# The order table covers the whole program, and the second 768-token block's output goes by seven products

## The chip, the cores and the metric

The kernel runs on one core of one Trainium2 chip. The metric is the device time of that core in microseconds, median of several runs. The engines named below are TensorE (PE, its weight loads PEld), VectorE (DVE), ScalarE (ACT), GpSimd (POOL) and SyncE (SP), whose queue issues nearly all DMA transfers.

## The reference

Attention over pooled keys and values, then a feed-forward layer with a gate:

```python
k_p = k.reshape(B, H, Sp, 8, D).mean(axis=3)      # 576 keys -> 72
v_p = v.reshape(B, H, Sp, 8, D).mean(axis=3)
scores = scale * np.matmul(q, k_p.transpose(0, 1, 3, 2))
scores = scores - np.max(scores, axis=-1, keepdims=True)
attn = np.exp(scores)
attn = attn / (np.sum(attn, axis=-1, keepdims=True) + 1e-09)
x = np.matmul(attn, v_p)                          # -> [4608 tokens, 512]
h = x @ w_in                                      # 512 x 2048
g = h * np.clip(h + 3.0, 0.0, 6.0) / 6.0
out = g @ w_out                                   # 2048 x 512
```

B = 8, H = 8, 576 positions, D = 64, all in fp32. q, k and v are 8 x 8 x 576 x 64.

## The kernel before, in words

**Numbers.** Each fp32 factor is split into a high and a low part in fp32r; a product is the sum of three matmuls (high by high, high by low, low by high).

**Blocks.** The 4608 tokens are cut into blocks of 512, 256, 384, 384 and eight of 384. The first four are plain: `Step` computes the first product, the gate and the second product for one f of 16 at a time (L825 and L856). The last eight are taken in pairs as four super blocks n = 0 to 3 of 768 tokens. Their first product goes by seven products of half-size matrices in place of eight (`PERIOD`; matmuls at L1113, 384 columns). Their second product, g by w_out, has two forms. `out_plain` (L1139 to 1180) runs 16 f x 6 tiles of 128 tokens x 3 = 288 matmuls of 512 columns (L1166). `out_seven` (L1182 to 1264) runs seven products (`KINDS`), each with 4 pieces m x 3 tiles x 6 = 72 matmuls of 256 columns (L1239), 504 in all, and adds the products up on VectorE (`mix` L1196 on the gate's values, `result` L1219 on the sums).

**Attention beside it.** While a super block runs, the attention of blocks ahead is done in steps between its matmuls: `load_q` (L235), `load_k` (L243), `load_v` (L278, L282), the pooling adds of v (L377, tile `vst`), scores (`product`, L456, TensorE), their maximum (`top`, L460, VectorE), exponentials (ScalarE), the transposes of the attention weights (L553, L562), their low parts (`alo` L574, `arem` L585, VectorE) and the product with v (L632).

**Weights.** All weights of the super blocks go through DRAM tables and come back in chunks of 512 KB: `chunk` (L977) keeps up to seven in two rings, wsFalse with four buffers and wsTrue with three; a chunk is issued on SyncE's queue, in order, once a buffer is free. Tables are wd (first product, 28 chunks), w2d (w_out plain) and w2t (w_out combined for seven products). The w2t tables are made from w2d chunks by `combine(n, i)` (L992 to 1009), eight times in all: on VectorE two sums of 128x512 (L1000), four of 128x256 (L1003), on ScalarE the high part (L1005), on VectorE the low part (L1006), then two stores of 512 KB (L1009). Its two tiles, `th` and `tq`, have two buffers together (`NREL`). A combine runs in an `out_plain`, where `MAKE[n]` names it. Each part that the second product multiplies is split in `split_g` (ScalarE L1093, VectorE L1094; tile `part`, three buffers).

**What sets the order.** `ORDER` holds, for each engine, a list of numbers: the instructions traced in a window of the program, in the order in which they must go. `put_in_order` makes each depend on the one before (no semaphore is added within an engine). The window covers the first block; the tile scheduler orders what follows by its own costs. Three rules stand beside it: what is behind the window waits for its last instruction; `mark` and `after_mark` keep loads and pooling work behind the last gate, part or chunk load; `last_h` keeps the first matmuls of a second product behind the last of the first product.

```python
SEVEN = (2, 3)
MAKE = ((0, 1, 2, 3), (4, 5, 6, 7), (), ())
...
            for x, y in zip(numbers, numbers[1:]):
                behind(mine[y], mine[x].name)
            last[engine] = mine[numbers[-1]].name
```

Of the kernel before, what the change touches and what calls it, by code (L numbers as in the profile page):

```python
# [45 lines left out]
SEVEN = (2, 3)  # L46
MAKE = ((0, 1, 2, 3), (4, 5, 6, 7), (), ())
# [8 lines left out]
        0-12 17-18 13-16 19-23 34-55 60-63 66-67 56-59 64-65 70-73 68-69 74-78 24-27 88-89 79-81 90-95 28-30  # L56
        98-99 82-84 96-97 85-87 31 110-111 106-109 32-33 112-118 128-136 119-121 221-224 122-127 103-105 100-102
        137-154 240-243 155-157 256-257 158-166 176-181 167-169 173-175 276-277 170-172 203-205 194-199 182-190
        200-202 206-208 191-193 228-233 209-211 218-220 287-288 307-308 212-214 309 225-227 215-217 234-239
# [4 lines left out]
        438-440 409 451-453 464-466 441-443 426-428 467-472 454-456 422-425 489-491 476-478 444-447 486-488  # L64
        479-482 457-460 473-475 492-503 483-485 546-547 513-515 504-506 540-542 572-573 554-556 507-509 557-559
        543-545 548-550 592-593 551-553 510-512 522-524 519-521 560-565 525-527 516-518 566-568 528-533 586-588
        569-571 574-579 589-591 534-536 594-599 580-582 537-539 583-585
    """,
    "DVE": """
        3 2 1 0 4-8 87 11 15 9 12 17 16 10 18 13 19 14 20-21 23 22 24 26 34 28 40 64 29 25 61 32 30 33 62 36 35  # L70
        37 27 39 38 47 31 43-44 41 65 55 93 45 50 49 51 63 52-53 56 54 42 48 59-60 57-58 99 74 46 100 77 73 106
        76 75 79 81 78 82 111 80 107 121 86 108 83-84 112 67 110 85 113 90 88 109 89 68 94 114 91-92 115 131 96
        98 95 101 136 97 103 66 143 105 102 116 104 137 118 117 132 122 120 126 119 128 133 127 130 129 144 140
        123 138 147 139 142 141 72 149 145 70-71 146 124 69 152 125 135 148 151 150 154 156 134 159 153 157 155
        166 158 160-161 168 170 167 163 172 162 169 173 164-165 171 174-175 178-179 187 183 181 184-186 188 194
        176 189 182 177 190 199 191 180 200 192 201 193 195 197-198 202 196 203
    """,
    "Activation": """
        3 2 0-1 4-18 27 19 34 21 20 25 23 82 22 24 81 28-32 35-38 46 26 33 53 40-43 54 44 47-50 52 56 51 60 55
        39 59 69 89 61 57-58 45 88 74 96 95 71 67 70 75 68 97 104-107 98 72 76 79 73 80 77 108-111 86 78 83-84  # L80
        93 62 90 85 87 94 117-120 91 126-129 99 102 92 115 103 100 112 136 65 130 137 101 138-139 116 113 124
        121 114 125 122 140 123 143 66 63 131 64 132 134 144 135 153 133 145 141 147 142 150 148 146 154 151 149
        155 157 160 156 152 166 158 161 159 167 170-172 162-163 168 164 173 165 174 176 178 169 175 183 177
        180-181 179 187 186 184 188 185 194-197 189 202-205 198-199 182 200 208-211 190-191 201 206 192 207
        212-213 193
    """,
    "Pool": """
        0-1 12 2-3 18 4 7-8 10 5 9 6 14 13 16 15 17 11 19-20 24 21 23 22
    """,
    "SP": """  # L90
        2-3 1 0 4-5 8 6-7 14 9 11 10 22-24 21 20 13 12 15 18 16 19 25-26 28 31 17 27 32 34 33 29 41 30 44 51 35
        48 46 43 36 47 39 52 59 42 37-38 45 40 50 49 53-55 57-58 60 56
# [5 lines left out]
def attention_moe_kernel(  # L98
# [73 lines left out]
    marks = {}  # L172

    def mark():
        marks[traced[-1].engine] = traced[-1].name

    def after_mark():

        if len(window) == 2 and traced[-1].engine in marks:
            behind(traced[-1], marks[traced[-1].engine])  # L180

    def put_in_order():

        a, b = window
        last = {}
# [4 lines left out]
        for name, text in ORDER.items():  # L190
# [36 lines left out]
    def load_q(tile):  # L227

        qtiles[tile] = []
        for i, (b, s0, n, _) in enumerate(tile):  # L230
# [5 lines left out]
            after_mark()  # L236
# [4 lines left out]
    def load_k(b, p):  # L241
        kraw[b, p] = ring("kst")
        nc.sync.dma_start(kraw[b, p], k[b, p])  # L243
        after_mark()
# [3 lines left out]
    def prep_k(b, p):  # L248
# [12 lines left out]
        after_mark()  # L261
# [9 lines left out]
    def load_v(b, p):  # L271
# [5 lines left out]
        if p < NPAIR:  # L277
            nc.sync.dma_start(to, v[b, p : p + 2, :, half].rearrange("c r n -> r c n"))  # L278
            after_mark()
            return  # L280
        for c in range(3):
            nc.sync.dma_start(to[c * REM : (c + 1) * REM], vr[b, :, :, half].rearrange("g r n -> r g n"))  # L282
            after_mark()
# [86 lines left out]
    def prep_v(b, p):  # L370
# [441 lines left out]
    class Step:  # L812
# [104 lines left out]
    def sums_of(i, h):  # L917
# [4 lines left out]
        for r, w in enumerate(pair_of(i)):  # L922
# [3 lines left out]
            after_mark()  # L926
# [38 lines left out]
    def chunk(n, ahead=NSTREAM - 1):  # L965

        while (m := len(loaded)) <= n + ahead and m < len(chunks):
# [10 lines left out]
            mark()  # L978
# [13 lines left out]
    def combine(n, i):  # L992
# [5 lines left out]
        for r in range(2):  # L998
            w = next_w2(n, 2 * i + r).bitcast(F32)
            nc.vector.tensor_tensor(out=q[:, 2 * r : 2 * r + 2], in0=w[:, :, 0], in1=w[:, :, 1], op=ALU.add)  # L1000
            after_mark()
        for to, a, b, how in ((3, 3, 1, ALU.subtract), (1, 1, 0, ALU.subtract), (0, 0, 3, ALU.add), (2, 2, 0, ALU.subtract)):
            nc.vector.tensor_tensor(out=q[:, to], in0=q[:, a], in1=q[:, b], op=how)  # L1003
            after_mark()
        nc.scalar.copy(hi.bitcast(F32R), q)  # L1005
        nc.vector.tensor_tensor(out=q.bitcast(F32R), in0=q, in1=hi, op=ALU.subtract)  # L1006
        after_mark()
# [48 lines left out]
    def super_block(n, j, first_att, second_att):  # L1056
# [10 lines left out]
        def gate(src, i, k):  # L1067
# [9 lines left out]
            mark()  # L1077
# [13 lines left out]
        def split_g(key, src):  # L1091
# [3 lines left out]
            mark()  # L1095
# [35 lines left out]
        last_h = next(i for i in reversed(traced) if i.engine == mybir.EngineType.PE).name  # L1131
# [4 lines left out]
        (out_seven if n in SEVEN else out_plain)(n, j, bank, parts, split_g, split_f, pairs, second_att, rest, last_h)  # L1136
        assert not rest

    def out_plain(n, j, bank, parts, split_g, split_f, pairs, att, rest, last_h):  # L1139
# [5 lines left out]
        for f in range(NF):  # L1145
# [5 lines left out]
            for t in range(NT2):  # L1151
# [393 lines left out]
```

## Time and profile before

| What | Value |
|---|---|
| runs | 906.92, 903.03, 901.94 us; median 903.03 |
| profiled execution: span | 903.1 us (no other time of it is given) |
| PE busy | 878.2 us (97%), 5144 records |
| PEld busy | 810.2 us (90%) |
| DVE busy | 642.1 us (71%), 1307 |
| ACT busy | 541.5 us (60%), 1498 |
| POOL busy | 85.3 us (9%), 168 |
| DMA moved | 193.67 MB, 214 GB/s on average |
| chain that ended last | PE 86%, DMA 8%, DVE 4%, ACT 1%, issue 1% |

Super blocks run from about 342 us on; their second products lie at 422 to 495, 571 to 642, 714 to 780 and 839 to 903 us. A busy time counts matmuls as busy until a modelled end, so a full PE says only that it was always given work. The granted clock (PEclk) is a share of full speed, 2.4 GHz; 0.5 is 1.2 GHz. DMA is the mean busy share of 16 DMA engines.

### The profile page before, as it was taken

How to read it: one execution, taken by the hardware profiler on the slowest of the kernel's cores; microseconds unless marked ns; L12 is line 12 of the kernel's file. 1: busy time of each engine (PE TensorE's matmuls, PEld its weight loads, DVE VectorE, ACT ScalarE, POOL GpSimd, SP SyncE). 2: the span in 40 equal slices, each digit the busy share in tenths (PEclk: the TensorE clock that was granted, in tenths of full speed). 3: DMA queues.
4: the chain of work that ended last, by engine and by line, in shares of the span. 5: the costliest groups of instructions: out<-in, count | busy, mean ns of one | idle time of the engine just before them, and what ended most of it. 6: DMA issues, size and time to landing. Idle time of an engine off the chain costs nothing.

```text
span 903.1 us, 15089 instructions
## 1 busy us (share of the span) xinstructions
PE 878.2 (97%) x5144; PEld 810.2 (90%) x5144; DVE 642.1 (71%) x1307; ACT 541.5 (60%) x1498; POOL 85.3 (9%) x168
## 2 busy tenths in 40 slices
PE   7999999999999999998999998999999999999998
PEld 7788888988999999997888998788999999999998
DVE  6999855576966784976765766468588877466664
ACT  5998666665657564874443767345477856355442
POOL 4100002210202010211000201000110200000000
PEclk9999999999999999998999999999999999999999
DMA  9970207995425147975865877556896777877873
GB/s 304 391 273 0 94 1 238 366 316 147 112 70 159 50 136 231 362 236 175 262 210 173 270 243 242 176 182 210 267 340 218 218 243 239 279 238 233 280 262 132
DMA packets 120588, 193.67 MB, mean 214 GB/s; under 512 B 12992, under 2 KB 79296, under 8 KB 120512
## 3 DMA queue, kind: packets, MB, share of 16 engines
q1 hardware_dynamic: 120368, 192.71, 65.6%
q8 instruction: 41, 0.67, 0.3%
q14 instruction: 35, 0.29, 0.1%
q10 hardware_dynamic: 144, 0.00, 0.0%
HBM read 151.78 MB, written 40.89 MB: 213 GB/s over the span
## 4 chain that ended last, share of the span: by engine, by line
PE 86%; DMA 8%; DVE 4%; ACT 1%; issue 1%; SPq 0%; DVEq 0%; ACTq 0%
PE psx L1113 22%; PE psx L1166 15%; PE pso L856 14%; PE psh L825 13%; PE psx L1239 13%; PE psa L456 4%; PE psa L632 4%; PE psa L562 1%; DMA qt<-q_l 1%; DMA wsFalse<-wd 1%; DMA raw<-w_in_l 1%; DMA raw<-w_out_l 1%; DMA wsTrue<-wd 1%; DMA wd<-wq 1%; DMA vst<-v_l 1%
## 5 line engine op out<-in xcount | busy, mean ns | idle before, releaser
L1113 PE MATMUL psx<-x,wsFalse 128*128 128x384 f32 x768 | 151.1, 342 | 1.5 <-ACT c L1088 0.8
L825 PE MATMUL psh<-xhi,w 128*128 128x384 f32 (+2 forms) x520 | 146.1, 340 | 1.1 <-DVE g L837 1.1
L1113 PEld LDWEIGHTS psx<-x,wsFalse 128*128 128x128 f32 x768 | 135.1, 190 | 2.8 <-ACT c L1088 1.3
L1094 DVE TENSOR_TENSOR part<-g,part 128x768 fp32r<-128x768 f32 x88 | 84.5, 961 | 50.3 <-ACT part L1093 50.1
L856 PE MATMUL pso<-w,ghi 128*128 128x512 f32 x384 | 119.7, 398 | 0.0
L1113 PE MATMUL psx<-x,wsTrue 128*128 128x384 f32 x576 | 116.5, 345 | 0.7 <-DMA wsTrue<-wd 0.7
L1093 ACT CAST part<-g 128x768 fp32r<-128x768 f32 x88 | 73.7, 837 | 70.4 <-PE psx L1239 43.5
L1113 PEld LDWEIGHTS psx<-x,wsTrue 128*128 128x128 f32 x576 | 101.3, 191 | 1.7 <-DVE g L1074 1.3
L825 PEld LDWEIGHTS psh<-xhi,w 128*128 128x128 f32 x520 | 93.2, 188 | 8.4 <-DVE g L837 1.6
L464 ACT ACTIVATE e<-psa,mx 128x72 f32<-128x72 f32 x256 | 78.6, 326 | 23.7 <-DVE mx L460 22.9
L1166 PE MATMUL psx<-wsFalse,part 128*128 128x512 f32 x360 | 88.0, 400 | 0.0
L825 PE MATMUL psh<-xlo,w 128*128 128x384 f32 (+2 forms) x260 | 86.9, 335 | 0.0
L492 POOL TENSOR_TENSOR a<-e,sm 128x256 f32<-128x256 f32 x60 | 40.4, 674 | 471.6 <-DVE sm L481 356.0
L1166 PEld LDWEIGHTS psx<-wsFalse,part 128*128 128x128 f32 x360 | 67.4, 190 | 15.2
L1080 DVE TENSOR_TENSOR g<-psx,c 128x384 f32<-128x384 f32 x96 | 52.6, 553 | 37.6 <-PE psx L1113 25.8
L856 PEld LDWEIGHTS pso<-w,ghi 128*128 128x128 f32 x384 | 69.2, 188 | 10.5
L1073 ACT ACTIVATE r<-g,small 128x384 f32<-128x384 f32 x96 | 59.1, 626 | 32.3 <-DVE g L1080 30.0
L856 PE MATMUL pso<-w,glo 128*128 128x512 f32 x192 | 72.8, 397 | 0.0
L1239 PE MATMUL psx<-wsFalse,part 128*128 128x256 f32 x576 | 71.5, 281 | 0.2 <-ACT kept L1214 0.2
L1239 PEld LDWEIGHTS psx<-wsFalse,part 128*128 128x128 f32 x576 | 69.8, 189 | 0.6 <-ACT kept L1214 0.6
L1074 DVE SCALAR_TENSOR_TENSOR g<-r,g 128x384 f32<-128x384 f32 x96 | 54.8, 578 | 12.5 <-ACT r L1073 12.0
L1088 ACT COPY c<-psx 128x384 f32<-128x384 f32 x96 | 44.9, 484 | 31.2 <-PE psx L1113 30.8
(134 smaller groups left out, 1532.7 us busy)
## 6 DMA issues: line engine op xcount, KB each, us to landing
wsFalse<-wd SPq DMA_DIRECT2D x64, 512.0 KB, 4.5
wsTrue<-wd SPq DMA_DIRECT2D x48, 512.0 KB, 4.5
wsFalse<-w2d SPq DMA_DIRECT2D x36, 512.0 KB, 5.1
wsTrue<-w2d SPq DMA_DIRECT2D x20, 512.0 KB, 5.1
raw<-w_in_l SPq DMA_DIRECT2D x16, 512.0 KB, 8.5
raw<-w_out_l SPq DMA_DIRECT2D x16, 512.0 KB, 9.1
w2d<-w SPq DMA_DIRECT2D x32, 256.0 KB, 4.2
wd<-wq SPq DMA_DIRECT2D x64, 128.0 KB, 2.0
```

What stands on the lines that cost most here:

```text
L464: nc.scalar.activation(self.e[:, h], self.ps[:, h], AF.Exp, bias=self.mx[:, h : h + 1], accum_out=self.sm[:, h : h + 1])
L825: nc.tensor.matmul(self.ps, l[f][:, c, :], r[:, c, :], start=c == 0 and i == 0, stop=c == NCC - 1 and i == 2)
L856: nc.tensor.matmul(pos, l, r, start=f == 0 and i == 0, stop=f == NF - 1 and i == 2)
L1073: nc.scalar.activation(r, src, AF.Relu, bias=half_low, scale=GSCALE / (6.0 * WSCALE))
L1074: nc.vector.scalar_tensor_tensor(out=g_of[i][:, k], in0=r, scalar=GSCALE, in1=src, op0=ALU.min, op1=ALU.mult)
L1080: nc.vector.tensor_tensor(out=g_of[i][:, k], in0=ps, in1=kept, op=ALU.add)
L1088: nc.scalar.copy(c, ps)
L1093: nc.scalar.copy(t[:, 0], src)
L1094: nc.vector.tensor_tensor(out=t[:, 1], in0=src, in1=t[:, 0].bitcast(F32), op=ALU.subtract)
L1113: nc.tensor.matmul(ps, w[:, l, c * P : (c + 1) * P], t[:, r, c], start=o in (1, 2, 5) and c == 0 and k == 0, stop=c == 1 and k == 2, skip_ ...
L1166: nc.tensor.matmul(to, l, w[:, qs, r], start=f == 0 and k == 0, stop=end and k == 2)
L1239: nc.tensor.matmul(to, t[:, l, k, i * P : (i + 1) * P], w[:, k, r], start=begin and k == 0 and y == 0 and i % 2 == 0, stop=m == NM - 1 and ...
```

## The change

Super block 1's second product takes the form of seven products, so all eight combines are made in super block 0's second product, the only one that stays plain. The table `ORDER` is new and numbers the whole program (PE 0 to 5133, DVE 0 to 1339, Activation 0 to 1228, Pool 0 to 156, SP 0 to 560), `put_in_order` is always called, and the three rules beside it are gone.

```diff
-SEVEN = (2, 3)
-MAKE = ((0, 1, 2, 3), (4, 5, 6, 7), (), ())
+SEVEN = (1, 2, 3)
+MAKE = ((0, 1, 2, 3, 4, 5, 6, 7), (), (), ())
...
 ORDER = {
     "PE": """
-        0-12 17-18 13-16 19-23 34-55 60-63 66-67 56-59 64-65 70-73 68-69 74-78 24-27 88-89 79-81 90-95 28-30
...
+        0-12 21-33 17 13-16 18-20 34-48 50-53 49 54-55 60-61 56-59 62-63 66-67 64-65 70-73 68-69 74-79 90 88-89
...
-    marks = {}
-
-    def mark():
-        marks[traced[-1].engine] = traced[-1].name
-
-    def after_mark():
-
-        if len(window) == 2 and traced[-1].engine in marks:
-            behind(traced[-1], marks[traced[-1].engine])
-
     def put_in_order():
 
         a, b = window
-        last = {}
...
                 behind(mine[y], mine[x].name)
-            last[engine] = mine[numbers[-1]].name
-        for i in traced[b:]:
-            if i.engine in last and on(i, i.engine):
-                behind(i, last[i.engine])
...
-        last_h = next(i for i in reversed(traced) if i.engine == mybir.EngineType.PE).name
...
-                        if f == 0 and k == 0:
-                            behind(traced[-1], last_h)
...
-                        if begin and k == 0 and y == 0:
-                            behind(traced[-1], last_h if i % 2 == 0 else opened)
-                            opened = traced[-1].name
...
             if j == 1 and u == 3:
-                window.append(len(traced))
                 paced.add_more()
...
-    if ORDER:
-        put_in_order()
+    window.append(len(traced))
+    put_in_order()
```

Every call of `mark()` and `after_mark()` goes as well. Lines of the changed kernel stand 131 to 141 higher: L456 becomes L596, L562 L702, L585 L725, L377 L518, L977 L1115, L235 L381, L278 L421, L1000 L1137, L1009 L1143, L1094 L1227, L1166 L1297, L1239 L1368.

TensorE's instructions go from 4918 to 5134 (288 fewer of L1166, 504 more of L1239), VectorE's from 1307 to 1340, ScalarE's from 1214 to 1231, SyncE's from 547 to 561 (12 more chunk loads and 8 more stores of out, 6 fewer of the plain form). The 56 copies of weights into wd and w2d, which SyncE issued at once after block 1 had begun, now stand between the stores of wq in blocks 2 and 3. At the start, all 26 fillers (`busy`, L320) stand ahead of the first scores, where 13 did and the other 13 came in between later.

VectorE at the end of super block 0's first product, before. `g6_4649` is a gate's value of that product, `psa_4927` the transposed attention weights, `vst_4757` a load of v, `tq_4912` the first combine:

```order
L585 TENSOR_TENSOR arem_4806<-psa_4927,arem_4806 32x128
L377 TENSOR_TENSOR vst_4757<-vst_4757,vst_4799 128x512
L460 TENSOR_REDUCE mx_4971<-psa_4973 128x4
L585 TENSOR_TENSOR arem_4933<-psa_4927,arem_4933 32x128
L377 TENSOR_TENSOR vst_4757<-vst_4757 128x2x128
L1080 TENSOR_TENSOR g6_4649<-psx_4787,c_4836 128x384
```

The same place with the change:

```order
L725 TENSOR_TENSOR arem_4806<-psa_4927,arem_4806 32x128
L620 TENSOR_SCALAR sm_4840<-sm_4840 128x4
L621 RECIPROCAL sm_4840<-sm_4840 128x4
L725 TENSOR_TENSOR arem_4933<-psa_4927,arem_4933 32x128
L1208 SCALAR_TENSOR_TENSOR g6_4649<-r_4871,psx_4650 128x384
L1208 SCALAR_TENSOR_TENSOR g6_4649<-r_4750,g6_4649 128x384
L1213 TENSOR_TENSOR g6_4649<-psx_4787,c_4836 128x384
L600 TENSOR_REDUCE mx_4971<-psa_4973 128x4
L714 TENSOR_TENSOR alo_4805<-psa_5004,ahi_4804 128x2x64
L1213 TENSOR_TENSOR g6_4649<-psx_4788,c_4836 128x384
L1208 SCALAR_TENSOR_TENSOR g6_4649<-r_4892,g6_4649 128x384
L518 TENSOR_TENSOR vst_4757<-vst_4757,vst_4799 128x512
```

The second `arem` went from behind the `vst` add, which waits for two loads, to ahead of it; the gates of the last pieces went ahead of it too.

SyncE at the end of super block 1's first product, before (`wd27` is the last chunk of that product, `w2d0` the first ones of the second, `qt` the next tokens of q):

```order
L977 DMA wsFalse_6165<-wd27_119 128x1024
L977 DMA wsFalse_6189<-w2d0_120 128x1024
L235 DMA qt_6199<-q_l 128x4x128
L278 DMA vst_6201<-v_l 128x2x256
L977 DMA wsFalse_6229<-w2d0_120 128x1024
L977 DMA wsTrue_6250<-w2d0_120 128x1024
L278 DMA vst_6252<-v_l 128x2x256
L977 DMA wsTrue_6289<-w2d0_120 128x1024
L235 DMA qt_6299<-q_l 128x4x128
```

And with the change:

```order
L1115 DMA wsFalse_6213<-wd27_119 128x1024
L381 DMA qt_6247<-q_l 128x4x128
L381 DMA qt_6347<-q_l 128x4x128
L1115 DMA wsFalse_6237<-w2d0_120 128x2x512
L1115 DMA wsFalse_6277<-w2d1_121 128x2x512
L1115 DMA wsTrue_6298<-w2d2_122 128x2x512
L1115 DMA wsTrue_6337<-w2d3_123 128x2x512
L421 DMA vst_6249<-v_l 128x2x256
```

Both loads of q now stand ahead of the chunks of the second product, where the second stood behind four of them.

VectorE in super block 0's second product with the change, from the seventh combine (`tq_5456`) to the first row of the eighth (`tq_5527`), with the last part (`part_5521`):

```order
L1137 TENSOR_TENSOR tq_5456<-wsTrue_5216 128x512
L1137 TENSOR_TENSOR tq_5456<-wsTrue_5221 128x512
L1139 TENSOR_TENSOR tq_5456<-tq_5456 128x256 x4
L1227 TENSOR_TENSOR part_5521<-g6_4649,part_5521 128x768
L1155 TENSOR_TENSOR x5_5440<-x_5118,x5_5440 128x768
L1163 TENSOR_TENSOR x_4525<-x_4525 128x768
L1155 TENSOR_TENSOR x6_5469<-x_4525,x6_5469 128x768
L1141 TENSOR_TENSOR tq_5456<-tq_5456,th_5455 128x1024
L1155 TENSOR_TENSOR x3_5475<-x_5118,x3_5475 128x768
L1137 TENSOR_TENSOR tq_5527<-wsFalse_5300 128x512
```

Before, this stage held four combines, and the parts behind them were the same 16; now the last part stands behind the beginning of the seventh.

## Rows read from the trace of the kernel before

**Rows 1.** windows by stage: PE, PEld, DVE, ACT, POOL busy, clock, DMA share, GB/s.

```profile
140.00:218.00 78.00, 76.35 (x458) 69.07 (x456) 49.59 (x133) 45.98 (x166) 12.79 (x27) 1.00 0.89 289
422.00:495.00 73.00, 73.00 (x339) 60.23 (x339) 46.88 (x82) 28.55 (x58) 2.57 (x4) 0.99 0.64 204
571.00:642.00 71.00, 71.00 (x320) 58.23 (x319) 46.33 (x79) 30.20 (x61) 2.58 (x6) 1.00 0.63 199
714.00:780.00 66.00, 65.80 (x541) 65.59 (x541) 48.63 (x68) 34.32 (x62) 2.58 (x4) 1.00 0.77 249
```

**Rows 2.** chain of waits, second products: start, duration (us), work.

```profile
472.63 21.87 PE psx L1166 x95
...
619.76 22.25 PE psx L1166 x96
...
839.22 59.46 PE psx L1239 x498
```

**Rows 3.** TensorE's waits: total us, times, longest.

```profile
PE psa L456 <- DMA qt<-q_l: 4.5, 2, 3.9
PE psa L562 <- DVE arem L585: 4.3, 1, 4.3
...
PE psa L456 <- DMA stage<-q_l: 1.5, 1, 1.5
```

**Rows 4.** windows after the two stops (columns as in rows 1).

```profile
417.00:424.00 7.00, 6.20 (x19) 5.84 (x20) 5.62 (x16) 3.83 (x15) 0.86 (x2) 0.51 0.35 97
567.10:570.60 3.50, 3.50 (x14) 3.41 (x13) 1.99 (x6) 2.03 (x10) 0.00 (x0) 0.51 0.29 68
```

**Rows 5.** timeline of VectorE, end of super block 0's first product.

```profile
412.62 0.28 DVE L585 TENSOR_TENSOR arem<-psa,arem 32x128 fp32r<-32x128 f32 x1
416.27 0.69 DVE L377 TENSOR_TENSOR vst<-vst 128x512 f32<-128x512 f32 x1 [3.37 <-DMA vst<-v_l]
...
417.36 0.29 DVE L585 TENSOR_TENSOR arem<-psa,arem 32x128 fp32r<-32x128 f32 x1
```

**Rows 6.** chain of waits, loads in it.

```profile
15.76 9.92 DMA raw<-w_in_l
...
408.55 7.60 DMA vst<-v_l
...
552.27 5.36 DMA qt<-q_l
...
560.38 5.71 DMA qt<-q_l
```

**Rows 7.** timeline of VectorE, rows of combines in both second products.

```profile
423.42 1.28 DVE L1000 TENSOR_TENSOR tq<-wsFalse 128x512 f32<-128x512 f32 x2
424.74 1.80 DVE L1003 TENSOR_TENSOR tq<-tq 128x256 f32<-128x256 f32 x4
427.71 1.22 DVE L1006 TENSOR_TENSOR tq<-tq,th 128x1024 fp32r<-128x1024 f32 x1 [1.17 <-ACT th L1005]
...
433.20 1.29 DVE L1000 TENSOR_TENSOR tq<-wsFalse 128x512 f32<-128x512 f32 x2
...
445.02 1.28 DVE L1000 TENSOR_TENSOR tq<-wsTrue 128x512 f32<-128x512 f32 x2
...
454.89 0.69 DVE L1000 TENSOR_TENSOR tq<-wsTrue 128x512 f32<-128x512 f32 x1 [0.29 <-DMA w2t<-th]
...
623.79 1.28 DVE L1000 TENSOR_TENSOR tq<-wsFalse 128x512 f32<-128x512 f32 x2
...
639.85 1.28 DVE L1000 TENSOR_TENSOR tq<-wsFalse 128x512 f32<-128x512 f32 x2
```

**Rows 8.** line L1009 (stores of combines): issue to landing.

```profile
DMA to landing us min/median/max: 3.2/5.5/7.6
```

**Rows 9.** timeline of TensorE at the start.

```profile
2.38 5.53 PE L320 MATMUL idle<-ident 128*128 128x128 f32 x26 [2.38 <-POOL ident masks.py:199]
```

**Rows 10.** costliest groups by line: busy, mean ns, idle before.

```profile
L1239 PEld LDWEIGHTS psx<-wsFalse,part 128*128 128x128 f32 x576 | 69.8, 189 | 0.6 <-ACT kept L1214 0.6
```

More of the change, by code (lines that the diff above doesn't have):

```diff
@@ new lines @@
+        1706-1707 1590-1603 1605-1606 1608-1609 1604 1607 1610-1624 1626-1627 1629-1630 1740-1741 1625 1628
+        1631-1645 1647-1648 1650-1651 1646 1649 1652-1673 1694-1695 1674-1675 1677-1678 1676 1679-1682 1696-1699
+        1728-1731 1683-1684 1686 1685 1687-1691 1732-1733 1708-1713 1700-1705 1714-1725 1734-1739 1742-1759
+        1762-1773 1777-1788 1726-1727 1760-1761 1789-1794 1797-1808 1795-1796 1809-1814 1774-1776 1823-1828
+        1817-1822 1831-1836 1815-1816 1837-1842 1849-1851 1843-1848 1852-1857 1872-1883 1858-1866 1829-1830
@@ new lines @@
+        2537-2538 2516-2518 2498-2503 2531-2536 2539-2544 2551-2552 2559-2564 2553-2558 2525-2530 2591-2593
+        2565-2570 2612-2613 2579-2584 2545-2550 2600-2611 2585-2590 2571-2572 2614-2619 2669-2671 2573-2578
+        2653-2655 2647-2652 2594-2599 2626-2633 2635-2639 2634 2640 2657-2662 2620-2625 2679-2681 2663-2668
+        2682-2684 2701-2706 2641-2646 2707-2712 2656 2672 2717-2719 2685-2694 2720-2722 2713-2716 2673-2678
+        2735-2736 2755 2749-2754 2756 2695-2700 2729-2734 2737-2742 2757-2762 2777-2782 2723-2728 2763-2768
@@ new lines @@
+        2795-2800 2775-2776 2827-2828 2743-2748 2783-2788 2769-2774 2807-2808 2880-2881 2789-2794 2801-2806
+        2809-2820 2829-2834 2821-2826 2835-2869 2882-2883 2926 2870-2879 2884-2889 2902-2903 2927 2890-2899
+        2904-2909 2920-2921 2910-2919 2922-2925 2928-2929 2940-2941 2930-2935 2900-2901 2936-2939 2942-2947
+        2961-2962 2973 2948-2951 2955-2960 2963-2972 2974 2952-2954 2975-2988 3002-3003 2989-2998 3004-3009
+        3020-3021 3010-3019 3022-3025 3030-3031 3042-3043 3026 3052-3053 3064-3065 3032-3041 3044-3047 3054-3063
@@ new lines @@
+        3066-3071 3086-3087 3072-3075 3080-3085 3088-3091 3027-3028 3092-3093 3108-3109 2999-3001 3132-3133
+        3144-3145 3094-3103 3110-3115 3126-3127 3116-3125 3128-3131 3134-3143 3146-3151 3162-3163 3152-3161
+        3164-3169 3180-3181 3170-3179 3182-3186 3029 3187 3198-3199 3188-3197 3200 3048-3051 3201-3203 3076-3079
+        3204-3215 3222-3226 3104-3107 3216-3221 3227-3257 3348-3349 3258-3259 3270-3271 3356-3357 3276-3277
+        3288-3289 3260-3269 3272-3275 3350-3355 3278-3287 3290-3295 3306-3307 3296-3305 3308-3313 3324-3325
@@ L68 @@
+        5128-5133
     """,
     "DVE": """
[L70 to L74, printed above, removed]
@@ L93 @@
+        520 519 521-538 541 539 542-546 540 547-555 557 556 558-560
     """,
@@ L1135, in super_block, with out_plain @@
         att_banks[:] = ["a0", "a1"]
-        (out_seven if n in SEVEN else out_plain)(n, j, bank, parts, split_g, split_f, pairs, second_att, rest, last_h)
+        (out_seven if n in SEVEN else out_plain)(n, j, bank, parts, split_g, split_f, pairs, second_att, rest)
         assert not rest
-    def out_plain(n, j, bank, parts, split_g, split_f, pairs, att, rest, last_h):
+    def out_plain(n, j, bank, parts, split_g, split_f, pairs, att, rest):
         NT2 = 2 * HALF // P
@@ L1180, in out_plain, with out_seven @@
                 paced.upto(len(paced.steps))
-    def out_seven(n, j, bank, parts, split_g, split_f, pairs, att, rest, last_h):
+    def out_seven(n, j, bank, parts, split_g, split_f, pairs, att, rest):
         NT2, NM, W2 = HALF // P, NF // 4, DM // 2
```

196 lines of the change are left out of this document (163 added, 33 removed).

## Prediction, made before the changed kernel ran

> **What bounds the kernel now.** I read the windows by stage first. TensorE is busy nearly all the time: 73.00 of 73.00 us in super block 0's second product, 71.00 of 71.00 in super block 1's, 65.80 of 66.00 in super block 2's, which already goes by seven products; VectorE has 46.9, 46.3 and 48.6 us of work there [rows 1]. So time falls only if TensorE gets less work or loses fewer of its stops. The chain of waits gives the price of its work: 95 matmuls of L1166 (512 columns) in 21.87 us and 96 in 22.25, so 230 to 231.8 ns each, and 498 of L1239 (256 columns) in 59.46, so 119.4 ns [rows 2]. TensorE's waits give its stops: only two are over 2 us inside the program, 4.3 us for VectorE's `arem` (one wait) and 4.5 us for `qt` loads (two waits, 3.9 the longer) [rows 3]. After each, the granted clock is at its lower level for a while: 0.51 between 417 and 424 us, 0.51 between 567.1 and 570.6 [rows 4]. That is 1.2 instead of 2.4 GHz, each time right after TensorE had stood about 4 us.
>
> The forecast is made against the profiled span, 903.1 us; no other time of that execution is given, and the median of the runs is 903.03, so the two may be taken as one.
>
> **1. Seven products in super block 1.** Removed: 16 f x 6 token tiles x 3 = 288 matmuls at 231.8 ns = 66.8 us. Added: 7 kinds x 4 x 3 x 6 = 504 at 119.4 ns = 60.2 us. Both lie on the path, since TensorE is busy 71.00 of 71.00 us there. **-6.6 us.** The products break even at 66.8 / 504 = 132.5 ns each, so between no gain and -6.6 the row of super block 2 and 3's own products decides, and it says -6.6. The 12 more chunk loads (6.3 MB) and the extra VectorE sums are covered as in super block 2: there the same stage runs at DMA share 0.77 with TensorE idle only 0.2 us, VectorE at 48.6 of 66 [rows 1].
>
> **2. The stop at the end of super block 0's first product.** VectorE's own rows show its cause: `arem` at 412.62, then the pooled add `vst` which sat 3.37 us until its load came, and only then, at 417.36, the second `arem` on which the transposed attention matmuls (L562) waited [rows 5]. The load was issued at 408.55 and took 7.60 us [rows 6]. In the new order the second `arem` stands three short rows behind the first, and the `vst` add eight rows behind that. It then ends near 413.5 instead of 417.65, so all but a few tenths of the 4.3 us go. With the stop I expect the half clock to go: 6.20 us of TensorE work at 0.51 would take 3.2 at full clock, so 3.0 to 3.2 more [rows 4]. **-7.0 us**; ends 0 (something else is late there) and -7.5. What is late next: the `vst` add still waits until about 416, and behind it stand the gates of `g6` and the first combine. None feeds TensorE at once: three parts are made beforehand (18 matmuls, 4.2 us, each), so the next one, behind the first combine, is due 12.5 us into the second product.
>
> **3. The stop at the end of super block 1's first product.** The second `qt` load was issued at 560.38 and landed 5.71 us later; the first at 552.27, 5.36 [rows 6]. Between them stand four chunk loads whose issue waits for buffers. Now both `qt` loads stand right behind the last chunk of the first product, so the second goes out about when the first did: landing near 558 instead of 566, eight us earlier against a wait of 3.9. The chunks that it passes (four of 512 KB) are first used when the second product starts, ten us on, and land in 5 to 6. **-6.0 us**: 4.5 of waits and 3.5 x 0.49 = 1.7 of half clock [rows 3, 4], less 0.2; ends 0 and -6.2.
>
> **4. The eight combines in super block 0.** Four move there from super block 1. One costs VectorE 1.28 + 1.80 + 1.22 = 4.3 us [rows 7], so its load in that stage goes from 46.9 to 64.1 of 73 us, and in super block 1 falls: no bound by work. But combines share two buffers: the next may not write until a store of the one before has landed, 3.2 to 7.6 us after its issue [rows 8]. Starts in this stage lay 9.8, 11.8 and 9.9 us apart, when nothing forced them closer [rows 7]. By my count of the new VectorE rows they must come every 9 us on average, and the last part is made just after the seventh combine begins: six spacings plus about 4.5 us, due at 15 x 4.2 + 4 us of attention work = 66.5. That leaves 10.3 us per spacing; the mean of the three is 10.5, the longest, 11.8, would make it 6 x 1.5 = 9 us late. I take **+1**, nearest to the mean; ends 0 and +9.
>
> **5. The rest.** Blocks 1 and 2: between 140 and 218 us TensorE lacks 1.65 us of 78.00, while DMA is at 0.89 with the copies of the weights [rows 1]; these move later, into blocks at a lower share, and I take **-1.2** (ends 0 and -1.65). Start: 13 more fillers go ahead of the first scores. The 13 that stand there now are 26 records and took 5.53 us [rows 9]; at that pace the scores come 5.5 us later at most, of which the `q` wait of 1.5 absorbs a part [rows 3]. The chain runs there through the load of `w_in` until 25.68 [rows 6], which covers most of the rest; I take **+0.5** (ends -1 and +3). The removed rules issue nothing. Super blocks 2 and 3 keep their work, and I count nothing there.
>
> Sum: -6.6 - 7.0 - 6.0 + 1 - 1.2 + 0.5 = -19.3, so 903.1 - 19.3 = **883.8 us**.
>
> **Rivals.** *Only the work falls.* A table is an order, no promise of arrival: the two stops may come back at another load, since the same loads are issued by the same queue, and the gains of 2 and 3 go. Against it: the rows that wait are known and each moved past its blocker. Time: 903.1 - 6.6 = 896.5, by the small terms 896 to 899. Chance 0.17.
>
> *The combines become the bound (slower).* With a store behind chunk loads that wait for TensorE, and TensorE waiting for parts behind the next combine, the spacing grows. One spacing of 16.1 us is on record in super block 1 (623.79 to 639.85) [rows 7]. At that, the last part is 6 x (16.1 - 10.3) = 35 us late: 883.8 - 1 + 35 = 918. It decides from 10.3 us on, and passes the time of before at about 13.6. For it: eight in one stage; against: VectorE waited only 0.29 us at the tightest start here (454.89), and the 16.1 fell where the table left them apart. Chance 0.05.
>
> *The small products are held by their weight loads (slower).* A load of 128x128 weights takes 189 ns [rows 10], longer than a 256-column product's 119.4. If they did not overlap, 504 x 0.189 = 95.3 us replace 66.8: +28.5 instead of -6.6, 919 in all. The rows of L1239 speak against it: 119.4 with one load each [rows 2]. The Trainium skill, "TensorE: Matmul & The Clock Gate", section "Back-to-back issue gap", says that in a stream of load and matmul pairs both set the spacing, about 81 ns at 128 columns and 131 at 512; an estimate on a straight line between these is 98 at 256, so 504 of them would take 49.2 us against 37.7 for 288, 11.5 longer, and the change would lose. The trace disagrees with both figures (119.4 and 231.8 ns), and the measurement decides. Chance 0.02.
>
> **How the numbers follow.** The forecast's case has 0.76, with 877 to 893 as its own range (below: all lower ends make 880, and 3 more for waits under a microsecond that a whole new order may close; above: the late parts' +9). The range reaches to the first rival, up to 898; outside lie the slower cases and a little on each side. This kernel's measurement tells about 0.5%, 4.5 us, from no change: 898.5 to 907.5. Faster: 0.76 and 0.12 of the first rival, 0.88; same 0.06; slower 0.06.
>
> **What would show it.** Right: L1239 with 1512 matmuls near 119 ns and super block 1's second product near 64 us; no wait over 1 us of the transposes (L562, in the changed kernel L702) on `arem`, nor of the scores (L456, now L596) on `qt`; clock at 1.0 from start to end of the super blocks; VectorE near 64 us in super block 0's second product with TensorE still full. Wrong: a row below 0.9 of TensorE in that product, a wait of its matmuls for parts, combines over 10.3 us apart, or a new stop of 4 us with 0.51 clock behind it elsewhere.

## The result and the profile after

| | before | changed |
|---|---|---|
| runs | 906.92, 903.03, 901.94, 905.54 us | 882.52, 880.2, 884.62, 886.76 us |
| median | 904.28 | 883.57 |
| profiled execution: span | 903.1 | 880.6 (its own time 882.52) |

The ratio is 0.9762, with a 95% interval of 0.9726 to 0.9798: 2.4% faster, 20.7 us by the medians and 22.5 by the two spans. A second set of runs gave 0.9745 (0.9721 to 0.9768). A run's time lies 1.7 to 2.2 us above the span of the same execution wherever both are on record, as 882.52 above 880.6 here.

First the windows by stage of the changed kernel, cut at its own stages (columns as in [rows 1]): block 1, super block 0's first and second product, super block 1's first and second, super block 2's second.

```profile
140.00:218.00 78.00, 78.00 (x470) 71.29 (x469) 53.95 (x143) 50.36 (x178) 9.58 (x22) 1.00 0.35 104
342.00:413.70 71.70, 71.70 (x429) 70.81 (x428) 55.07 (x124) 54.05 (x171) 9.38 (x18) 1.00 0.85 287
413.70:486.20 72.50, 72.50 (x342) 59.92 (x341) 65.23 (x118) 33.20 (x66) 3.15 (x6) 1.00 0.78 245
486.20:552.00 65.80, 65.80 (x395) 65.48 (x394) 51.62 (x109) 49.99 (x164) 11.97 (x21) 1.00 0.84 284
552.00:621.00 69.00, 66.93 (x533) 66.69 (x534) 58.23 (x94) 39.30 (x87) 3.73 (x8) 0.98 0.79 262
695.00:759.00 64.00, 64.00 (x529) 63.94 (x528) 50.66 (x63) 33.02 (x51) 0.87 (x2) 1.00 0.78 247
```

TensorE is full, at a clock of 1.00, in five of the six. Both places that held the old stops are clean: super block 0's first product runs into its second at 413.6 and super block 1's at 554.1 without a hole. Only 552 to 621 lacks 2.07 us and has a clock of 0.98. That is the new stretch, super block 1's second product by sevens. VectorE carries 65.2 us in super block 0's second product (46.9 before, [rows 1]), as four more combines should give.

TensorE's waits of the changed kernel, the four longest:

```profile
PE idle L461 <- POOL ident masks.py:199: 2.4, 1, 2.4
PE psx L1368 <- ACT part L1226: 2.1, 1, 2.1
PE psa L772 <- DVE a L694: 1.4, 2, 1.2
PE psa L772 <- ACT x L774: 1.3, 1, 1.3
```

The 4.5 us on `qt` and the 4.3 us on `arem` of [rows 3] are gone. What leads now inside the super blocks is one wait of 2.1 us for a part.

The chain of waits gives the price of the work again, a piece of super block 0's second product and super block 3's:

```profile
464.56 20.67 PE psx L1297 x90
...
817.20 60.19 PE psx L1368 x504
```

That is 229.7 and 119.4 ns per matmul, against 231.8 and 119.4 in [rows 2]. All 504 products of 256 columns took 60.2 us, the figure of the prediction.

Where the time went is read from the timeline of TensorE: the first matmul of each stage, before,

```profile
341.72 0.51 PE L1113 MATMUL psx<-x,wsFalse 128*128 128x384 f32 x2
...
422.10 2.10 PE L1166 MATMUL psx<-wsFalse,part 128*128 128x512 f32 x5
...
570.79 1.56 PE L1166 MATMUL psx<-wsFalse,part 128*128 128x512 f32 x6
...
713.84 2.42 PE L1239 MATMUL psx<-wsTrue,part 128*128 128x256 f32 x19
...
839.05 2.18 PE L1239 MATMUL psx<-wsTrue,part 128*128 128x256 f32 x17
```

and with the change:

```profile
340.36 0.51 PE L1245 MATMUL psx<-x,wsFalse 128*128 128x384 f32 x2
...
413.58 1.79 PE L1297 MATMUL psx<-wsFalse,part 128*128 128x512 f32 x7
...
554.05 2.17 PE L1368 MATMUL psx<-wsFalse,part 128*128 128x256 f32 x17
...
695.27 1.94 PE L1368 MATMUL psx<-wsFalse,part 128*128 128x256 f32 x15
...
817.03 2.17 PE L1368 MATMUL psx<-wsFalse,part 128*128 128x256 f32 x17
```

The differences from one stage to the next, beside the terms of the prediction that fall into it (a stretch runs from the first matmul of one stage to that of the next, so the fourth holds super block 1's second product and super block 2's first):

| stretch, up to the start of | gained, us | forecast |
|---|---|---|
| super block 0's first product | 1.36 | 1.2 - 0.5 = 0.7 |
| its second product | 7.16 | 7.0 |
| super block 1's second product | 8.22 | 6.0 - 1 = 5.0 |
| super block 2's second product | 1.83 | 6.6 |
| super block 3's second product | 3.45 | 0 |
| the end (903.1 and 880.6) | 0.5 | 0 |
| sum | 22.5 | 19.3 |

The two stops gave what they should, and a little more. The seven products gave much less than 6.6 in their stretch, and later stretches that were counted at nothing gave nearly as much back. Part of both is not time but work that moved: the windows of the attention alone (tile `psa`), the fourth and the fifth stretch, before and then with the change. In brackets behind TensorE's busy time stands the number of its matmuls; clock, DMA share and GB/s are again of the whole stretch.

```profile
570.79:713.84 143.05, 22.15 (x136) 19.50 (x136) 14.94 (x42) 28.56 (x138) 1.00 0.72 233
713.84:839.05 125.21, 5.65 (x28) 4.06 (x28) 3.16 (x9) 5.62 (x22) 1.00 0.77 247
...
554.05:695.27 141.22, 25.40 (x151) 21.65 (x151) 17.59 (x49) 32.11 (x155) 0.99 0.80 261
695.27:817.03 121.76, 3.77 (x16) 2.54 (x16) 1.00 (x3) 2.81 (x7) 1.00 0.77 253
```

Fifteen more attention matmuls stand in the fourth stretch and twelve fewer in the fifth. Taken from each one's start to the start of the next matmul, and without the waits, they fill 1.2 us more of the one and 1.4 us less of the other.

The rest of what the fourth stretch lacks has its cause in the timelines between 579 and 592 us. SyncE, VectorE and ScalarE there:

```profile
579.51 0.85 SPq L388 DMA_DIRECT2D kst<-k_l  x2
```

```profile
586.92 0.75 DVE L402 TENSOR_REDUCE ksum<-kst 128x72 f32<-128x576 f32 x1 [0.61 <-DMA kst<-k_l]
587.59 0.95 DVE L1227 TENSOR_TENSOR part<-g,part 128x768 fp32r<-128x768 f32 x1
```

```profile
587.71 0.53 ACT L410 ACTIVATE kbd<-ksum 64x72 f32<-64x72 f32 x2 [3.02 <-DVE ksum L402]
588.26 0.83 ACT L1226 CAST part<-g 128x768 fp32r<-128x768 f32 x1
```

A load of k goes out at 579.51 and lands 7.4 us later. VectorE's sum of it stands in the table at that place and waits 0.61 us; VectorE was 9.9 of 10 us busy from 570 to 580. ScalarE's `kbd` waits for the sum, idle for 3.02 us, and the cast of the next part stands behind it. TensorE waits 2.1 us for that part, and the window behind it ran at the lower clock for a while:

```profile
580.00:590.00 10.00, 7.93 (x66) 7.70 (x66) 9.22 (x13) 4.76 (x9) 0.00 (x0) 1.00 0.96 313
590.00:600.00 10.00, 10.00 (x74) 10.00 (x73) 7.57 (x15) 6.25 (x14) 0.31 (x1) 0.83 0.74 248
```

A clock of 0.83 over 10 us costs 1.7 us; with the wait, 3.8 of the 6.6 are spent again, and with the moved attention 5.0. It is the same kind of stop as the two that the change removed, only shorter. The clock's part is of this execution: when the changed kernel was profiled a second time, the wait was 1.7 us, the clock behind it stayed at 1.00, and the stretch took 140.6 us.

### The profile page after: what moved, and what is told of

Read it like the earlier page. It is cut to its first block, busy times and chain, and to the rows that moved or that the text cites. A ratio compares the mean times of both kernels' runs of the same rounds, so it can differ in the third digit from the quotient of the medians.

```text
span 880.6 us, 15638 instructions
## 1 busy us (share of the span) xinstructions
PE 866.7 (98%) x5360; PEld 814.2 (92%) x5360; DVE 677.3 (77%) x1340; ACT 555.9 (63%) x1515; POOL 86.2 (10%) x168
## 4 chain that ended last, share of the span: by engine, by line
PE 91%; DVE 5%; DMA 2%; ACT 1%; issue 1%; POOL 0%; ACTq 0%; DVEq 0%; POOLq 0%
PE psx L1245 26%; PE psx L1368 17%; PE psh L965 15%; PE pso L995 15%; PE psx L1297 8%; PE psa L596 4%; PE psa L772 4%; PE psa L702 1%; PE idle L461 1%; DMA kst<-k_l 1%; DMA vst<-v_l 1%; DVE part L1227 1%; DVE u L889 0%; DVE g L1325 0%; ACT part L1226 0%
## 5 line engine op out<-in xcount | busy, mean ns | idle before, releaser
L1226 ACT CAST part<-g 128x768 fp32r<-128x768 f32 x100 | 83.7, 837 | 67.6 <-PE psx L1368 56.9
L1227 DVE TENSOR_TENSOR part<-g,part 128x768 fp32r<-128x768 f32 x100 | 96.1, 961 | 32.5 <-ACT part L1226 31.2
L1245 PE MATMUL psx<-x,wsTrue 128*128 128x384 f32 x576 | 114.1, 340 | 0.0
L1368 PE MATMUL psx<-wsFalse,part 128*128 128x256 f32 x864 | 109.7, 284 | 0.0
L1368 PEld LDWEIGHTS psx<-wsFalse,part 128*128 128x128 f32 x864 | 107.1, 191 | 0.2 <-ACT kept L1343 0.2
L1368 PE MATMUL psx<-wsTrue,part 128*128 128x256 f32 x648 | 82.2, 284 | 2.1 <-ACT part L1226 2.1
L632 POOL TENSOR_TENSOR a<-e,sm 128x256 f32<-128x256 f32 x60 | 44.2, 737 | 407.6 <-DVE sm L621 310.7
L1368 PEld LDWEIGHTS psx<-wsTrue,part 128*128 128x128 f32 x648 | 79.4, 191 | 2.3 <-ACT part L1226 2.3
L995 PEld LDWEIGHTS pso<-w,ghi 128*128 128x128 f32 x384 | 69.2, 188 | 10.4
L1207 ACT ACTIVATE r<-g,small 128x384 f32<-128x384 f32 x96 | 58.2, 620 | 16.8 <-DVE g L1213 13.7
```

Of the source, the lines that this page charges most:

```text
L995: nc.tensor.matmul(pos, l, r, start=f == 0 and i == 0, stop=f == NF - 1 and i == 2)
L1207: nc.scalar.activation(r, src, AF.Relu, bias=half_low, scale=GSCALE / (6.0 * WSCALE))
L1226: nc.scalar.copy(t[:, 0], src)
L1227: nc.vector.tensor_tensor(out=t[:, 1], in0=src, in1=t[:, 0].bitcast(F32), op=ALU.subtract)
L1245: nc.tensor.matmul(ps, w[:, l, c * P : (c + 1) * P], t[:, r, c], start=o in (1, 2, 5) and c == 0 and k == 0, stop=c == 1 and k == 2, skip_ ...
L1368: nc.tensor.matmul(to, t[:, l, k, i * P : (i + 1) * P], w[:, k, r], start=begin and k == 0 and y == 0 and i % 2 == 0, stop=m == NM - 1 and ...
```

## Experiments

Apart from the seven products alone, and one repeat, all are the changed kernel with a few rows of its table moved, so each edit is shown by the instructions that it moves, with the lines of the changed kernel. In their profiles lines stand 4 to 6 lower, because the table is set in other lines. Medians are compared with the changed kernel's 883.57 us; the ratio is to the kernel before. Differences of a few us between medians are blurred by the start: in the seven profiles of this section and of the result whose rows up to there are the same, super block 0 begins between 339.9 and 343.6 us. From there on the stretches repeat closely, so where it helps a stretch is given as well: with the new order super block 0's first product takes 73.2 us in every profile that leaves its rows alone, and the stretch behind it 140.5 to 140.9.

**One row of VectorE back.**

```diff
 L621 RECIPROCAL sm_4840
+L518 vst_4757<-vst_4757,vst_4799
 L725 arem_4933<-psa_4927,arem_4933
...
-L518 vst_4757<-vst_4757,vst_4799
```

> The changed kernel with one VectorE row put back: at the end of super block 0's first product the vst add (L518) stands ahead of the second arem (L725) again. Theory (the stop came from this one row): in the changed kernel the add has its loads at 414.5 us, so the arem ends near 415.5 instead of 410.05; TensorE stands about 4 us after 411.4, and its clock is at the lower level for some us after that. +7 us: 890.5 against 883.6, with a wait on arem near 4 us and a window of 0.5 clock behind it. Rival (the loads now come early enough, or TensorE has other work there): under 1.5 us, 883.6 to 885.

Measured 888.63 us (ratio 0.981, 0.9779 to 0.9841): 5.1 us slower. The wait and the clock are back; TensorE's wait, VectorE's timeline and the window after it:

```profile
PE psa L697 <- DVE arem L720: 4.5, 1, 4.5
```

```profile
412.30 0.28 DVE L720 TENSOR_TENSOR arem<-psa,arem 32x128 fp32r<-32x128 f32 x1
...
417.94 0.69 DVE L513 TENSOR_TENSOR vst<-vst 128x512 f32<-128x512 f32 x1 [4.95 <-DMA vst<-v_l]
418.67 0.29 DVE L720 TENSOR_TENSOR arem<-psa,arem 32x128 fp32r<-32x128 f32 x1
```

```profile
417.00:424.00 7.00, 4.90 (x17) 4.84 (x18) 4.13 (x10) 2.44 (x11) 0.00 (x0) 0.53 0.08 31
```

One row among 1340 makes the stop, as the first theory says; the rival falls. The size was 5.1 by the medians, whose intervals overlap, where 7 was expected. In the profile super block 0's first product takes 79.8 us (343.64 to 423.40) instead of 73.2: 6.5 us, close to the 7.

**One load of q back.**

```diff
 L381 qt_6247<-q_l
-L381 qt_6347<-q_l
 L1115 wsFalse_6237<-w2d0
 L1115 wsFalse_6277<-w2d1
 L1115 wsTrue_6298<-w2d2
 L1115 wsTrue_6337<-w2d3
+L381 qt_6347<-q_l
```

> The changed kernel with one SyncE row put back: the second load of q at the end of super block 1's first product stands behind four chunk loads of the second product again. Theory (the stop came from this load's place in the queue): it goes out about 8 us later, the scores wait for it some 4 us, and the lower clock follows: +6 us, 889.6 against 883.6, with a wait of L596 on qt near 4 us. Rival (the stop went with the whole new order, not with this row): no wait over 1 us, 883 to 885.

Measured 887.16 us (0.9801, 0.9766 to 0.9835): 3.6 us slower, and the wait is there:

```profile
PE psa L591 <- DMA qt<-q_l: 3.1, 1, 3.1
```

The place of this load in SyncE's queue made the second stop. It costs 3.6 by the medians, whose intervals overlap, where 6 was expected. In the profile its stretch takes 145.6 us (413.13 to 558.70) instead of 140.5, 5.1 more, and the stretch behind it 2.5 less: with the first `qt` load still early, the wait is one of 3.1 us, not two of 4.5 together, and in that execution the new wait for a part in the next product was 0.4 us instead of 2.1.

**The seven products alone.** The kernel before with two constants.

```diff
-SEVEN = (2, 3)
-MAKE = ((0, 1, 2, 3), (4, 5, 6, 7), (), ())
+SEVEN = (1, 2, 3)
+MAKE = ((0, 1, 2, 3, 4, 5, 6, 7), (), (), ())
```

> The kernel before with the two constants of the change alone (super block 1's second product by seven products, all eight combines in super block 0's), under the old table and the old rules. Theory (the work is worth 6.6 us wherever it stands, and the rest of the gain is the order): 904.3 - 6.6 = 897.7, with both old stops of about 4 us still there; if the eight combines under the scheduler's order cost their part, up to 906. Rival (the seven products carry most of the gain): 890 or less.

Measured 902.99 us (0.9976, 0.9957 to 0.9996): 1.2 us faster, not 6.6. In the profile both old stops are there and a third, 15 us into super block 0's first product:

```profile
PE psa L456 <- DMA qt<-q_l: 5.7, 2, 3.5
PE psa L562 <- DVE arem L585: 3.6, 1, 3.6
...
PE psx L1113 <- DMA wsTrue<-wd: 1.8, 1, 1.8
```

The work is 6.6 us less by the prices above, but `qt` is waited for 5.7 us instead of 4.5, and the 1.8 us are new. Under the old table and the scheduler's own order for the rest, most of the work's gain is waited away; the remainder of the change's 20.7 us needs the order. The profile shows where: the fourth and the fifth stretch gain 4.3 and 2.3 us, with the same moved attention (151 and 16 matmuls) and no wait over 0.3 us in the fourth, so the seven products do give nearly their 6.6 there. Super block 0's first product takes 2.8 us more, the stretch behind it 0.6, and super block 0 begins 1.4 later, which is within the spread of the starts. Both the theory (897.7) and its rival (890) missed; the upper end that the text left open (906) is nearer.

**The sum of k later.** Two moves that take ScalarE's stop away from the part.

```diff
-L402 ksum_6858<-kst_6574
 ...
 L725 arem_6532<-psa_6814,arem_6532
+L402 ksum_6858<-kst_6574
 L1227 part_6987<-g2_5790,part_6987
...
-L410 kbd1_84<-ksum_6858 x2
 L1226 part_6954<-g0_5590
 ...
 L543 vrem_6469<-vst_6570
+L410 kbd1_84<-ksum_6858 x2
 L1226 part_7013<-g4_5999
```

> The changed kernel with one VectorE row (the sum of k, L402, which waits 0.6 us for its load at 586.3) and the two ScalarE rows that use it (L410) put behind the next two parts in super block 1's second product. Nothing on TensorE needs them before 633 us. Theory (TensorE's only wait of 2.1 us inside the super blocks, and the lower clock after it, come from ScalarE standing at L410 ahead of a part): -2.1 and about -1.5 of clock, 880 against 883.6, no wait of L1368 on part. Rival (VectorE is the bound there, 9.9 of 10 us busy from 570 to 580): the wait comes back at a later part, 883 to 884.

Measured 881.7 us (0.9739, 0.9711 to 0.9766), 1.9 us less, half of what was expected, and by itself within the spread of the runs. The trace is clearer. The wait for ScalarE's part is gone, one of 0.6 us for VectorE's half of a later part is in its place, and the clock stays at 1.00:

```profile
PE psx L1363 <- DVE part L1222: 0.6, 1, 0.6
```

```profile
555.00:624.00 69.00, 68.04 (x547) 67.55 (x546) 59.77 (x97) 41.48 (x101) 5.05 (x9) 1.00 0.81 269
```

Idle time falls from 2.07 to 0.96 us, and the fourth stretch takes 139.6 us instead of 141.2. So the cause of the wait is shown, though not that of the clock, which stayed at 1.00 behind the same wait in other profiles too (last section). The rival has a share: VectorE, busy for 18.8 of the 20 us from 560 to 580 in the changed kernel, is the next to be late.

**Copies back to block 1.**

```diff
 L388 kst_1647<-k_l
 ...
 L421 vst_1998<-v_l
+L1073 wd0_92<-w_0_344 x2
+...
+L1073 w2d3_123<-w_15_1263 x2
 L381 qt_1902<-q_l
```

> The changed kernel with the 56 copies of weights (14.7 MB) put back to where SyncE issued them before: together, early in block 1, ahead of the stores of wq. Theory (TensorE's small waits in blocks 1 and 2 came from loads and stores behind that lump of copies): between about 140 and 225 us 1.5 to 3 us come back (the two traces differ by 2.85 there), 885 to 886.5 against 883.6. Rival (they came from the order of VectorE and ScalarE): under 0.5 us.

Measured 916.06 us (1.0132, 1.0108 to 1.0156): 32 us slower, which neither theory had. VectorE's wait, TensorE's, and SyncE's queue:

```profile
DVE ksum L396 <- DMA kst<-k_l: 32.6, 1, 32.6
```

```profile
PE psh L959 <- DVE g L971: 29.2, 1, 29.2
```

```profile
162.24 2.59 SPq L1067 DMA_DIRECT2D wd<-w  x3
...
202.35 3.04 SPq L1067 DMA_DIRECT2D w2d<-w  x4
...
207.07 0.88 SPq L382 DMA_DIRECT2D kst<-k_l  x2
```

The 56 copies hold the queue for 43 us, 0.77 us each, and the load of k that VectorE needs at 178.7 stands behind them. I had not counted the queue that the copies occupy. Nor was it the old place: before, the copies went out from 147 to 197 us, mixed with loads of q, k and v. A milder mix was tried next.

```diff
 L388 kst_1647<-k_l
+L1073 wd0_92<-w_0_344 x2
 L381 qt_1556<-q_l
+L1073 wd5_97<-w_1_486
+L1073 w2d0_120<-w_0_431
 L381 qt_1837<-q_l
...
```

> As copies_early, where 56 copies in a row took SyncE 43 us to issue (0.77 us each, 162 to 205 us) and a load of k behind them came 32.6 us late. Here the copies are mixed between the same loads: two behind each row up to the second load of k, then four. Theory (the queue's time per issue did the harm, not the bytes): the loss falls from 32 us to under 5; what is left in blocks 1 and 2, 1.5 to 3 us, is what early copies cost, 885 to 886.5. Rival (the transfers themselves collide): over 10 us lost again.

Measured 900.48 us (0.9925, 0.9898 to 0.9951): still 17 us slower than the changed kernel. Now VectorE waits for another transfer that the copies push back, the stores and loads around `wq`:

```profile
DVE wq L1057 <- DMA wd<-wq: 11.7, 2, 8.6
```

That is the rival's size, over 10 us, but its mechanism, transfers that collide, is not shown: once issued, the stores of `wq` land in 2.0 us (median; 2.1 in the changed kernel). They are issued late, behind copies in the queue. What early copies alone cost the kernel before, whose other rows fitted them, these two runs don't tell: they show only that the new order can't have them there.

**Fillers spread again.** The second 13 fillers go back among the scores, the transposes and the first products.

```diff
-L461 idle<-ident x26
+L461 idle<-ident x13
 ...
+L461 idle<-ident x3
 ...
```

> The changed kernel with the second 13 fillers (L320 of before, L461) put back among the scores and the first products. Theory (the start hangs on loads, the fillers cover empty time): within 1 us of 883.6 either way, first products at the same time within 0.5. Rival (fillers ahead of the scores cost their 2.8 to 5.5 us): 878 to 881.

Measured 881.01 us (0.9746, 0.9726 to 0.9767): 2.6 us less by the medians. That interval and the changed kernel's overlap, and the start differs by 0.7 us in the traces, less than executions with the same rows there differ among each other (the run with one row of VectorE back begins super block 0 3.3 us later than the changed kernel). Open by itself.

**Stores of combines later**, by one chunk load and by two: a direct try of the prediction's slower rival.

```diff
 L1115 wsTrue_4863<-w2d1
-L1143 w2t0_124<-th_4911
 L1115 wsTrue_4883<-w2d1
+L1143 w2t0_124<-th_4911
```

> The changed kernel with the two stores of each of the first six combines one chunk load later in SyncE's queue (chunk loads wait for TensorE). It measures the rival of the prediction: combines too far apart. Theory (a spacing over 10.3 us makes parts late): the spacing grows from 9.2 to 11 to 13 us, VectorE waits at L1137 for the stores, TensorE waits for parts, +4 to +15 us: 888 to 899. Rival (there is slack in the stores, and the spacing is set by the table alone): spacing below 10.3, under 1 us more.

> As stores_later, with each store of the first six combines two chunk loads later instead of one. With one, the spacing went from 9.2 to 9.7 us on average and the time did not move. Theory (10.3 us is where parts begin to be late): the spacing goes to 11 to 13 us, TensorE waits for parts, 6 x (spacing - 10.3), so +4 to +16 us: 888 to 900. Rival (the threshold lies elsewhere, or combines catch up): below 886 although the spacing is over 10.3.

With one, 883.82 us (0.9776, 0.9755 to 0.9797), with two, 886.36 (0.9776, 0.9752 to 0.98). In the second, VectorE's timeline has its longest spacing (13.8 us) with a wait for a store, and the eighth combine starts where the stage ends:

```profile
426.75 1.29 DVE L1132 TENSOR_TENSOR tq<-wsFalse 128x512 f32<-128x512 f32 x2
440.59 1.29 DVE L1132 TENSOR_TENSOR tq<-wsTrue 128x512 f32<-128x512 f32 x2 [4.18 <-DMA w2t<-th]
...
486.37 1.29 DVE L1132 TENSOR_TENSOR tq<-wsFalse 128x512 f32<-128x512 f32 x2 [0.52 <-DMA w2t<-th]
```

The mean spacing of the seven is (486.37 - 417.92) / 7 = 9.8 us, so the threshold of 10.3 was not reached and stays untested; no matmul of L1297 waited. What came instead I had not listed: copies of finished sums (L1301) stand behind the eighth combine on VectorE, and the next first product waits 1.5 us for their banks; the stretch takes 143.4 us instead of 140.5. The first median is the changed kernel's, the second lies 3.4 us above the 882.99 that the changed kernel gave beside it (below), with intervals that overlap.

**Fixes together.** The sum of k later and, at the end of block 0, one cast of ScalarE behind three copies that TensorE waits for:

```diff
 L774 x_998<-psa_1171
-L913 w_15_1263<-u_1200
 L774 x_998<-psa_1219
 L774 x_998<-psa_1269
 L774 x_998<-psa_1234
+L913 w_15_1263<-u_1200
```

> The run with the sum of k later, and one more row: at the end of block 0 ScalarE's cast of w (L913), which waits for VectorE at 118.6 us, goes behind the three copies of x (L774) that TensorE waits for (1.3 us at 119.5). Theory: another -1.4 us, 880.3 against 881.7, no wait of L772 on x. Rival (the copies of x are late through TensorE's own order, or block 1 takes the gain back): 881.7.

Measured 880.08 us (0.9737, 0.9713 to 0.9762), and the wait of 1.3 us is out of the list. No wait is left in the fourth stretch, which takes 137.8 us, 5.3 less than before: the 6.6 without the 1.2 of attention that moved in. With the fillers spread as well, beside the changed kernel on the same chip:

> The changed kernel once more, unaltered, beside the next three: 883.6, between 880 and 887, ratio 0.976. It tells how far the others differ from it on one chip.

> The run with both fixes (sum of k later, cast of w behind the copies of x) and the second 13 fillers spread as in fillers_spread. Theory (the three act in different stages and add up): 883.6 - 1.9 - 1.6, and 0.7 to 2.5 for the fillers, 877.5 to 879.5. Rival (spreading the fillers is worth nothing): 880.

The changed kernel gave 882.99 us (0.9745, 0.9721 to 0.9768), the three fixes 878.0 (0.9683, 0.9663 to 0.9703). The intervals don't touch: 5 us, 0.6%, and better than both kernels. Its list of TensorE's waits for parts holds 0.6 and 0.5 us in place of 2.1 (1.7 in the changed kernel's second profile).

## Why the prediction was right, and where it was off

The time, 883.8 against 883.57, agrees better than its terms do, and the closeness is luck. The sum starts from a span, 903.1, and its result was met by a median of times, which lie about 1.9 us above their spans; the two may not be taken as one. Span against span the gain was 22.5 us and not 19.3, so 880.6 where 883.8 was forecast; by the medians it was 20.7. Inside the sum a term that came out 4.8 too small was made up by stretches that had been counted at nothing.

**1, the seven products (-6.6; 1.83 in its stretch).** The work has the size that was worked out: 119.4 ns and 60.2 us. The step that failed is the cover, "covered as in super block 2". In super block 1 the same stage runs beside more attention: VectorE has 58.2 of 69 us, not 48.6 of 66, with 18.8 busy of the 20 us before 580 and 9.2 of the next 10. The row that broke it was no work at all but a load of k, waited for in order. The list of signs named waits for parts, but for super block 0's second product; here it was the clock, expected at 1.0 throughout, that failed. The price was 3.8 us in the profiled execution, 1.7 of it clock. Another 1.2 us are the fifteen attention matmuls that moved into the stretch. Under the old table the cover did hold: the run of the seven products alone has no such wait there.

**2, the first stop (-7.0; 7.16).** Right in cause and size; the row put back alone brought a wait of 4.5 us and cost 6.5 in its stretch, 5.1 by the medians. The `vst` add, named as late next, waited 0.80 us at 414.55 and held nobody up.

**3 and 4, the second stop and the combines (-6.0 and +1; 8.22).** Right in cause. The `qt` waits went; the load put back brought 3.1 us of them and cost 5.1 in its stretch. The combines cost nothing rather than 1. VectorE's starts of combines in the changed kernel, the first, the second, and the last two:

```profile
416.16 1.29 DVE L1137 TENSOR_TENSOR tq<-wsFalse 128x512 f32<-128x512 f32 x2
...
424.74 1.29 DVE L1137 TENSOR_TENSOR tq<-wsFalse 128x512 f32<-128x512 f32 x2
...
470.91 1.28 DVE L1137 TENSOR_TENSOR tq<-wsTrue 128x512 f32<-128x512 f32 x2
...
480.38 1.29 DVE L1137 TENSOR_TENSOR tq<-wsFalse 128x512 f32<-128x512 f32 x2 [0.87 <-DMA w2t<-th]
```

That is 64.2 us for seven spacings, 9.2 each, under the 10.3 and under the 10.5 that I took from before's three (15 x 4.2 + 4 is 67 and not 66.5, so the 10.3 is rather 10.4). The one wait for a store, 0.87 us, is at the eighth, behind the last part. The rest of the 8.22 is 0.9 us of the first stop's lower clock, which in the kernel before reached past 422, 0.5 of a wait for a chunk in super block 1's first product, and about 0.3 of three attention matmuls (124 before, 121 after); some 0.3 us stay open.

**5, the rest (-0.7; 1.36, and 3.95 in super blocks 2 and 3).** Block 1 has no idle time left (78.00 of 78.00 us, against 76.35 in [rows 1]). Of this, 1.3 us is paid before it, in the wait for ScalarE's copies at the end of block 0, which no term had. The start's 0.5 can't be read: it differs by more between executions. The mis-sized term is the nothing for super blocks 2 and 3, which gave 3.95 us. They did not keep their work: with super block 1's second product by sevens, twelve of super block 2's attention matmuls, 1.4 us, already stand in the stretch before, and under the old table too, where the fifth stretch gains 2.3 us. Another 1.2 us are small waits that went, the longest of 0.6 us. The rest, 1.3 us, is spread over the matmuls of both super blocks, and no experiment took it apart.

**The rivals.** "Only the work falls" was wrong the other way round: the work alone, run by itself, gave 1.2 us of 6.6, because the old order lost the rest at other places, and the new order carried the change. The combines never bound. The weight loads did not hold the small products, and 119.4 ns again speaks against the straight line between the two figures that the Trainium skill, "TensorE: Matmul & The Clock Gate", gives in its section "Back-to-back issue gap"; it has none at 256 columns, so only the 231.8 at 512 disagrees with a figure itself, 131.

## What to carry to other kernels

In a program whose engines run in a fixed order, look for the row that waits for a transfer and ask what stands behind it on its engine: one such row cost 3.6 to 5.1 us here when it was put back (5.1 to 6.5 in its own stretch), though the add runs for 0.7 and the load's issue takes 0.6. Count a change of work only together with the waits of its stage, since under the old order 6.6 us less work gave 1.2. When a stage gets more slots, count what else moves into it: attention that moved made one stretch look worse here and the next one better. Before moving transfers to an earlier place, count what the queue needs to issue them and which load of later rows would then stand behind.

## What the runs showed of the hardware

A lump of copies held the issuing queue for about as long as its bytes took. In the run with the copies early, 56 copies of 256 KB took 43 us to issue, 14.7 MB or 340 GB/s, and the window in the middle of it shows the DMA engines full:

```profile
180.00:200.00 20.00, 4.09 (x26) 3.27 (x24) 0.00 (x0) 0.00 (x0) 0.00 (x0) 0.71 1.04 341
```

In the changed kernel the same copies, spread from 250 to 336 us, never show, and block 1 runs at a DMA share of 0.35. The landing time of one such copy, 4.2 us before, says nothing of what stands behind it in the queue.

A stop of TensorE of about 2 us was followed by the lower clock in some executions and not in others. At the wait for a part in super block 1's second product the clock fell behind stops of 2.1 us (the changed kernel) and 1.9 (stores two chunk loads later), each time to 0.83 over the next 10 us; it stayed at 1.00 behind 2.4 (fillers spread), 1.7 (the changed kernel again) and 1.4 (stores one later). So one profile doesn't tell whether such a stop costs its length alone.
